# A delta-rule attention and SiLU feed-forward kernel: chunk 0's queries turned two batches ahead of their scores, V loaded one transfer later, joins, narrowing and first MLP pieces in another order

## The chip, the cores and the metric

The kernel runs on one core of one Trainium2 chip. A core has a matrix engine (TensorE, PE in the profile), a vector engine (VectorE, DVE), a scalar engine (ScalarE, ACT), a general engine (GpSimd, POOL) and SyncE (SP), which in this kernel issues nearly all transfers between memory (DRAM) and the core's on-chip memory. TensorE writes into accumulation banks (PSUM); the other engines copy from there. Each engine works through its own instructions in the order in which the program pinned them, and waits where an operand is not ready. The metric is the device time of one execution in microseconds (us); lower is better.

## The reference: what is computed

There are 4 batches of 8 heads, 768 tokens of 48 values each. Per head a state of 48 x 48 values runs over the tokens; keys are scaled to length one.

```python
for t in range(S):
    kt, vt, bt = (k_n[:, :, t], v[:, :, t], beta[:, :, t, None])
    y[:, :, t] = np.einsum('bhd,bhde->bhe', q[:, :, t], state)
    v_old = np.einsum('bhde,bhd->bhe', state, kt)
    state = state + bt[:, :, :, None] * np.einsum('bhd,bhe->bhde', kt, vt - v_old)
...
h = x @ w_in
g = h * (1.0 / (1.0 + np.exp(-h)))
return (g @ w_out).astype(np.float32)
```

`x` is `y` with the heads of a token side by side: 3072 tokens of 384 values. `w_in` is 384 x 2048, `w_out` 2048 x 384. The inputs of the attention are float32; the two weight matrices come in as float64.

## The kernel before: how the work is tiled and ordered

**Chunks.** The 768 tokens are taken in six chunks of 128. Inside a chunk the token-by-token recurrence becomes matrix work: the key products of the chunk form a triangular matrix for each head, which must be inverted; with the inverse, the value corrections, the outputs and the new state are all matmuls. Each chunk has two halves (`hf`) of 64 tokens, and the batches go in two groups (`g`) of two.

**Chunk 0** is prepared by code of its own. Keys are transposed on TensorE (`turn` with j = 0, L490) and their diagonal blocks multiplied (`first_blocks`, L1274). VectorE computes the key lengths (`norm_steps`); `beta_of` (L351) turns beta; `block_steps` (L435) makes the step sizes `pg`. Then `invert_first` solves 16 x 16 blocks by a chain of small VectorE operations and leaves two transposed tables, `low` (L680) and `up` (L684). While VectorE does that, TensorE makes the key scores of the four batches (`first_score`, L1291) and the query scores (`first_queries`, L1293): the latter transposes the queries of a batch (`turn` with j = 1, whose result ScalarE negates into `kq` at L500) and then multiplies keys by queries (`score`, L519), whose result ScalarE copies into `ap` (L534). GpSimd masks those (L1345).

**Which word stands where.** The loop at L1349 advances the inverse by a step and then runs the words of one entry of a list: `s2` is `first_score(2)`, `q0` is `first_queries(0)`, `b` is a filler matmul (`busy`, L338) that waits for the inverse's step at that place. A filler's result is not used. Since every engine has its own order, the place of a word among the inverse's steps, which are VectorE's, does not matter to TensorE; the order of the words does.

**Joins.** `joins(hf, between)` (L1367) puts the small inverses together in ten stages: `corner`, `turned`, `straight`, and the two merges (`merge_half`, L796), each for both groups. After each stage it calls the next entry of `between`: `sizes_0` finishes VectorE's table of key lengths, `sized` scales V of chunk 0 on GpSimd (L447) and begins a weight piece, `filled(n)` does n steps of narrowing, `begin_next` begins the next piece. The first half's joins are followed by `inner` (L830), `first_outputs` (L874), and then the first MLP matmuls (`hidden`, L1031).

**Weights.** Each matrix is taken in eight pieces of 768 KB. A piece is loaded raw (`fetch_w_in`, L285; `fetch_w_out`, L297) and narrowed from float64 to float32 in three steps: two on ScalarE when it is begun (L226, L227), one on VectorE (L231), and one on VectorE with one on GpSimd (L235, L239). `fill(n)` does n such steps in the order of the pieces.

**Transfers.** All loads stand in one line on SP's queue. `linked` makes a load wait until the load before it in line has landed. `load_v(0)` has eight loads of 96 KB (L191).

**The script.** From L1526 on the order of chunk 0's solving, chunk 1's preparation and the MLP is written out as words: `s` a step of solving chunk 0 and then 1, `f` a step of narrowing, `r` one MLP piece (six matmuls of L1031, or their counterpart in the second layer, L1066), `j` a step of the second half's joins, `T` and `q` turns of chunk 1's keys and queries, `p` chunk 1's scores, `g` and `i` chunk 1's inverse (VectorE, L617 and L622), `l` and `m` key lengths, `t` sums of weights, `b` beginning a piece, `W7`, `w2`, `w3` loads of weights, `v` and `k` loads of V and keys. After the script, chunks 1 to 5 are handled by the loop at L1530, which runs two fixed patterns and is left as it is.

Of the kernel before, what the change touches and what calls it, by code (L numbers as in the profile page):

```python
# [19 lines left out]
def kernel(  # L20
# [20 lines left out]
    T = 32  # L41
# [16 lines left out]
    A, CC, M = deque(("a0", "a1", "a2")), deque(("c0", "c1", "c2")), deque(("m0", "m1"))  # L58
# [51 lines left out]
    def together(*parts):  # L110
        for _ in zip_longest(*parts):
            pass
# [12 lines left out]
    def on(e, hf, g):  # L125

        return HALVES[hf ^ e ^ g]
# [7 lines left out]
    def load_pair(to, src, c, bs):  # L135

        for g in range(bs.start // HB, bs.stop // HB):
            us = slice(HB * g, HB * (g + 1))
            for e, hf in ((g, None), (1 - g, 0), (1 - g, 1)):
                rows = slice(0, P) if hf is None else on(e, hf, g)  # L140
                tokens = slice(c * C, (c + 1) * C) if hf is None else slice(c * C + hf * W, c * C + (hf + 1) * W)
                in_line(nc.sync.dma_start(  # L142
                    out=to[rows, us, :, e, 0:D],
                    in_=src[us, e::2, tokens, :].rearrange("b h t d -> t b h d"),
                ))
# [25 lines left out]
    def linked(fetch, *args):  # L171

        pace.append(line[-1])
        fetch(*args)

    def load_k(c, bs=ALL):
        if c < NCH:
            load_pair(kbufs[c % 2], k, c, bs)
# [5 lines left out]
    def load_v(c):  # L184
        if c < NCH:
            vfs[c] = load.tile([P, 2, B, NP, D], FP32, name="vf", bufs=1)
            for hf in range(2):
                for g in range(2):
                    us = slice(HB * g, HB * (g + 1))
                    for e in range(2):  # L190
                        in_line(nc.sync.dma_start(  # L191
                            out=vfs[c][on(e, hf, g), hf, us],
                            in_=v[us, e::2, c * C + hf * W : c * C + (hf + 1) * W, :].rearrange("b h t d -> t b h d"),
                        ))
# [12 lines left out]
    for e in range(2):  # L207
        for g in range(2):
            to, of = slice(HH * e + HH // 2 * g, HH * e + HH // 2 * (g + 1)), slice(HH // 2 * g, HH // 2 * (g + 1))
# [66 lines left out]
    def fetch_w_in(i):  # L276
        if i in (0, 1, 6):
            raw = mlp.tile([P, SIZE], U32, name="raw", tag="gT", bufs=3)[:]
        elif i < 6:
            raw = room(i // 2 - 1, i % 2)  # L280
        else:
            raw = spare
        raw = raw.rearrange("p (a f) -> p a f", a=NKT)
        src = moe_w_in.rearrange("(a p) f -> p a f", p=P)[:, :, i * WF : (i + 1) * WF].bitcast(U32)
        in_line(nc.sync.dma_start(out=raw, in_=src))  # L285
        raws["in", i] = raw.rearrange("p a (f j) -> p a f j", j=2)
# [47 lines left out]
    def busy(n=1, after=None, how=NoSync):  # L334

        for _ in range(n):
            pw = bank(CC, "pw")
            done = pin(nc.tensor.matmul(  # L338
                pw[:, 0:DM], lhsT=ident[:],
                rhs=states[0][:].rearrange("p u a w -> p (u a w)")[:, 0:DM], start=True, stop=True,  # L340
            ))
            if after is not None:
                behind(done, after, how)
                after = None
# [4 lines left out]
    def beta_of(c):  # L349
        pb = bank(A, "pb")  # L350
        pin(nc.tensor.transpose(  # L351
            pb[:, 0:BH], beta_fm[:, c].rearrange("n s t -> n (s t)"), ident[0:BH, 0:BH]
        ))
        pin(nc.scalar.activation(
            out=beta_tok[:, c, :].rearrange("p (n e) -> p e n", e=2),
            in_=pb[:, 0:BH].rearrange("p (e n) -> p e n", e=2), func=ACTF.Copy,
        ))
# [125 lines left out]
    def turn(c, b, j, room, by_vector=False):  # L483

        if j == 0:
            kq_room(c, b)
        src, kq = (kbufs[c % 2], queries[c] if c < 2 else None)[j][:, b], kqs[c, b]
        pt = bank(room, "pt")
        for p in range(NP):
            pin(nc.tensor.transpose(  # L490
                pt[:, p * C : (p + 1) * C], src[:, p].rearrange("p e w -> p (e w)"), ident[:]
            ))
        ptv = pt[:].rearrange("p (a t) -> p a t", a=NP)
        if j == 1:
            if by_vector:
                pin(nc.vector.tensor_scalar(
                    out=kq[:, :, j, :], in0=ptv, scalar1=-1.0, scalar2=None, op0=ALU.mult
                ))
            else:
                pin(nc.scalar.mul(kq[:, :, j, :], ptv, -1.0))  # L500
        elif by_vector:
            pin(nc.vector.tensor_copy(out=kq[:, :, j, :], in_=ptv))
        else:
            pin(nc.scalar.copy(kq[:, :, j, :], ptv))

    def score(c, b, js, rooms, evacuate):

        g, u = b // HB, b % HB
        if (c, g) not in aps:
            aps[c, g] = {}  # L510
        for j in js:
            if j not in aps[c, g]:
                aps[c, g][j] = work.tile([P, HB, H, W], FP32, name=f"ap{j}", tag=f"ap{j}", bufs=2)
        ap, kq, n = aps[c, g], kqs[c, b], len(js)
        pa = [bank(room, f"pa{e}") for e, room in enumerate(rooms)]
        for p in range(NP):
            for e, hf in ((0, 0), (1, 1), (0, 1), (1, 0)):
                rows, half = slice(W * e, W * e + D), slice(W * hf, W * (hf + 1))
                pin(nc.tensor.matmul(  # L519
                    pa[e][half, p * n * W : (p + 1) * n * W], lhsT=kq[rows, p, 0, half],  # L520
                    rhs=kq[rows, p, js[0] : js[-1] + 1, half], start=True, stop=True,
                ))
        for e in range(2):
            of = pa[e][:, 0 : NP * n * W].rearrange("p (a j t) -> p a j t", a=NP, j=n)
            for i, j in enumerate(js):
                evacuate(j, e, ap[j][:, u, e::2, :], of[:, :, i, :])
# [6 lines left out]
    def by_act(to, of):  # L533
        return pin(nc.scalar.copy(to, of))  # L534
# [755 lines left out]

        score(0, b, (0,), (A, CC), evacuate)  # L1291

    def first_queries(b):  # L1293

        def evacuate(j, e, to, of):
            by_act(to, of)

        turn(0, b, 1, M)
        score(0, b, (1,), (A, CC), evacuate)

    busy(3)
    for b in range(B):
        square(0, b)
# [9 lines left out]
    for b in range(B):  # L1313
        add_squares(0, b)
    beta_of(0)
    for t in xis:
        pin(nc.gpsimd.memset(t, 0.0))
    first_sizes = norm_steps(0)
# [4 lines left out]
    pools["m0"] = pools["m1"] = ctx.enter_context(tc.tile_pool(name="hiddens", bufs=1, space=PSUM))  # L1323
    fetch_w_in(0)
    load_k(1)
    load_v(0)
    fetch_w_in(1)
    for c in range(1, NCH):
        beta_of(c)
    for b in range(2):  # L1330
# [3 lines left out]
    linked(load_q, 1)  # L1334
    fetch_w_in(4)
    linked(fetch_w_in, 3)
    linked(fetch_w_in, 5)
    linked(fetch_w_in, 6)
    begin(("in", 0))
    inv = invert_first(step)  # L1340

# [6 lines left out]

    for n in range(1 + Q):  # L1349
        done = next(inv)  # L1350
        for word in ["s2 s3", "", "q0", "", "q1", "", "q2", "", "", "q3", "", "", "b", "", "", "", "", "", ""][n].split():
            at = int(word[1:] or 0)
            if word[0] == "b":
                busy(1, done, Sync)
            elif word[0] == "s":
                first_score(at)
            elif word[0] == "q":
                first_queries(at)
            else:
                turn(1, at, 0, M)  # L1360
    corner, turned, straight = next(inv)
# [5 lines left out]
    def joins(hf, between=()):  # L1367

        for stage in (
            corner(0, hf), corner(1, hf), turned(0, hf), turned(1, hf), straight(0, hf), merge_half(0, hf, False),  # L1370
            straight(1, hf), merge_half(1, hf, False), merge_half(0, hf, True), merge_half(1, hf, True),
        ):
            yield from stage
            for what in between[:1]:
                what()
            between = between[1:]
# [4 lines left out]
    def filled(n):  # L1381
        return lambda: fill(n)
# [5 lines left out]
    def none():  # L1388
        pass

    together(joins(0, [none, sizes_0, sized, none, filled(2), none, filled(1), none, none, begin_next]))

    pieces = chained(hidden(0, 0), hidden(0, 1), project())

# [129 lines left out]
                pieces = chained(feed_forward(1, 0), feed_forward(1, 1))  # L1524

    for text in (  # L1526
        "s f2 s T f T s q b q T j5 j5 j16 f r j5 j8 j4 j16 j5 r q j20 b T f j8 j4 q W7 r j4 f2 j4 b j4 f j4 r j4 f2 j32 r e b j12 j8 f j4 j4 j4 j4 r j4 f j99 l h f2 l s b w2 f r l r l p r s w3 r l p r l2 p f l7 f2 s l b l f p r l5 s f l r l3 p f s2 l2 f l4 p f r2 f p g b p i v l p r f i r i2 r i l r i r b i2 r2 f b r i r3 i r f i b r2 i3 b b i2 r2 f2 i2 f r i r3 i r2 i r2 i r2 f i2 f i f r2 i f b f i4 r i b i r k f r z i r s r2 t r b z s b r f r m r s m r3 t r f2 t m r t f t m s m b r2 b s m3 r m s r m5 b c s m r m2 t s m r m t m2 b m2 r s m2 t m2",
    ):
        script(text)
    for c in range(1, NCH):  # L1530
# [59 lines left out]
```

## Time and profile before

| | |
|---|---|
| time, median of 3 runs | 656.09 us (652.70 to 657.33) |
| the profiled execution | 655.41 us |
| its span (first to last instruction) | 653.5 us |
| mean TensorE clock granted, as a share of full | 0.969 |
| busy: TensorE / VectorE / ScalarE / GpSimd | 631.4 / 391.6 / 216.2 / 95.4 us |
| moved by DMA | 53.68 MB, 82 GB/s on average |

Times in the profile count from the start of the span. A matmul of float32 shows as two records, each with a weight load. A row of the timeline gives start, duration, engine, line, operation, written tile `<-` read tiles, shape and count, and in brackets the idle time of that engine just before it with what ended it; "issue" means that nothing in the profile explains the idle time. In a row that merges several instructions the duration is that of the group. "SPq" is SP's queue: its rows are the issuing of transfers, not their landing. Tile names are those of the program's buffers, which are reused: `w_out<-in_moe_w_in_dram` is a raw piece of `w_in` parked in room that later holds `w_out`.

### The profile page before, as it was taken

How to read it: one execution, taken by the hardware profiler on the slowest of the kernel's cores; microseconds unless marked ns; L12 is line 12 of the kernel's file. 1: busy time of each engine (PE TensorE's matmuls, PEld its weight loads, DVE VectorE, ACT ScalarE, POOL GpSimd, SP SyncE). 2: the span in 40 equal slices, each digit the busy share in tenths (PEclk: the TensorE clock that was granted, in tenths of full speed). 3: DMA queues.
4: the chain of work that ended last, by engine and by line, in shares of the span. 5: the costliest groups of instructions: out<-in, count | busy, mean ns of one | idle time of the engine just before them, and what ended most of it. 6: DMA issues, size and time to landing. Idle time of an engine off the chain costs nothing.

```text
span 653.5 us, 21807 instructions
## 1 busy us (share of the span) xinstructions
PE 631.4 (97%) x9644; PEld 553.4 (85%) x9644; DVE 391.6 (60%) x902; ACT 216.2 (33%) x505; POOL 95.4 (15%) x96
## 2 busy tenths in 40 slices
PE   6879999999999999999999999999999999899997
PEld 4668788766789988989989989989989989789997
DVE  5844988997764986453987453987455964103112
ACT  1545847133342122451122452122451122341111
POOL 5232642146001020010020010020002000000000
PEclk9557999999999999999999999999999999999999
DMA  9763545340278424178424168424163024100101
GB/s 174 167 155 100 175 111 138 73 121 2 52 151 141 66 74 59 37 144 132 73 72 59 47 136 142 61 77 57 35 142 74 17 67 49 40 14 1 25 0 25
DMA packets 141310, 53.68 MB, mean 82 GB/s; under 512 B 112912, under 2 KB 134672, under 8 KB 141216
## 3 DMA queue, kind: packets, MB, share of 16 engines
q1 hardware_dynamic: 140880, 52.14, 39.4%
q8 instruction: 76, 1.25, 0.9%
q10 hardware_dynamic: 336, 0.15, 0.1%
q14 instruction: 18, 0.15, 0.1%
HBM read 39.62 MB, written 10.49 MB: 77 GB/s over the span
## 4 chain that ended last, share of the span: by engine, by line
PE 73%; DVE 9%; DMA 8%; SPq 5%; ACT 2%; issue 1%; POOL 0%; POOLq 0%; DVEq 0%
PE phid L1031 28%; PE px L1138 13%; PE py L1138 9%; PE po L1066 7%; DVE rank L617 4%; DVE x L622 3%; PE pz L830 3%; PE pa L519 3%; SPq L142 2%; DMA w_out<-in_moe_w_in_dram 2%; PE pu L850 2%; PE ph L818 2%; PE pyc L909 2%; DVE sums_of_g L1120 1%; DMA up<-x 1%
## 5 line engine op out<-in xcount | busy, mean ns | idle before, releaser
L1031 PE MATMUL phid<-xT,w_in 128*128 128x256 f32 x1152 | 258.4, 382 | 1.9 <-DMA xT<-part 1.9
L1031 PEld LDWEIGHTS phid<-xT,w_in 128*128 128x128 f32 x1152 | 215.8, 190 | 33.3 <-issue 3.5
L1041 ACT ACTIVATE gT<-phid 128x512 f32<-128x512 f32 x88 | 52.6, 597 | 145.8 <-PE phid L1031 143.6
L617 DVE SCALAR_TENSOR_TENSOR rank<-g,step,x 128x31 f32<-128x31 f32 (+15 forms) x124 | 49.7, 401 | 38.1 <-DMA g<-blocks 34.6
L1120 DVE TENSOR_TENSOR sums_of_g<-gT 128x384 f32<-128x384 f32 (+1 forms) x60 | 30.6, 529 | 58.4 <-ACT gT L1041 47.8
L1138 PE MATMUL py<-w_out,sums_of_g 128*128 128x192 f32 x320 | 56.8, 329 | 0.0
L1138 PE MATMUL px<-sums_of_w,sums_of_g 128*128 128x192 f32 x320 | 56.8, 329 | 0.0
L1138 PEld LDWEIGHTS px<-sums_of_w,sums_of_g 128*128 128x128 f32 x320 | 52.2, 190 | 0.5
L1138 PEld LDWEIGHTS py<-w_out,sums_of_g 128*128 128x128 f32 x320 | 52.2, 190 | 0.4
L622 DVE TENSOR_TENSOR x<-x,rank 128x31 f32<-128x31 f32 (+15 forms) x124 | 42.5, 343 | 4.3
L457 POOL TENSOR_TENSOR vf<-vf,n_slot 128x768 f32<-128x768 f32 x10 | 15.0, 1510 | 174.2 <-DMA vf<-in_v_dram 126.5
L478 DVE STREAM_TRANSPOSE kq<-stage 128x512 f32<-128x512 f32 x28 | 28.4, 1109 | 9.3 <-DMA stage<-in_q_dram 9.3
L534 ACT COPY xT<-pyc 48x128 f32<-48x128 f32 (+2 forms) x126 | 32.7, 260 | 1.6
L1138 PE MATMUL px<-sums_of_w,gT 128*128 128x192 f32 x160 | 28.4, 329 | 0.0
L1138 PE MATMUL py<-w_out,gT 128*128 128x192 f32 x160 | 28.4, 329 | 0.0
L1138 PE MATMUL px<-w_out,gT 128*128 128x192 f32 x160 | 28.0, 327 | 0.0
L830 PEld LDWEIGHTS pz<-vf,xi 64*64 64x64 f32 x768 | 25.0, 142 | 3.2 <-issue 2.9
L540 POOL COPY g<-x 64x256 f32<-64x256 f32 x4 | 5.0, 1242 | 152.6 <-DVE x L625 152.6
L519 PEld LDWEIGHTS pa<-kq 48*64 48x64 f32 x768 | 21.2, 161 | 7.0 <-ACT kq L500 4.4
L519 PE MATMUL pa<-kq 48*64 48x128 f32 (+1 forms) x768 | 24.3, 287 | 2.7 <-ACT kq L500 2.7
L1138 PEld LDWEIGHTS px<-w_out,gT 128*128 128x128 f32 x160 | 26.4, 190 | 0.5
L855 DVE TENSOR_TENSOR state<-state,pu 128x384 f32<-128x384 f32 x22 | 11.2, 551 | 26.0 <-PE pu L850 25.9
(197 smaller groups left out, 859.3 us busy)
## 6 DMA issues: line engine op xcount, KB each, us to landing
vf<-in_v_dram SPq DMA_DIRECT2D x48, 96.0 KB, 3.0
out_dram<-o SPq DMA_DIRECT2D x42, 96.0 KB, 2.2
w_out<-in_moe_w_in_dram SPq DMA_DIRECT2D x4, 768.0 KB, 5.4
sums_of_w<-in_moe_w_out_dram SPq DMA_DIRECT2D x4, 768.0 KB, 5.9
blocks<-ap SPq DMA_DIRECT2D x40, 64.0 KB, 1.9
g<-blocks SPq DMA_DIRECT2D x5, 512.0 KB, 3.5
kb<-in_k_dram SPq DMA_DIRECT2D x12, 192.0 KB, 4.4
kb<-in_k_dram SPq DMA_DIRECT2D x24, 96.0 KB, 4.5
```

The costliest lines, as they stand in the source:

```text
L457: pin(nc.gpsimd.tensor_tensor(out=vf, in0=vf, in1=of, op=ALU.mult))
L478: pin(nc.vector.transpose(out=kqs[c, b][:, :, j, :].rearrange("p a (i m) -> p a m i", i=T), in_=src.rearrange("p a (m d) -> p a m d", d=D) ...
L519: pin(nc.tensor.matmul(pa[e][half, p * n * W : (p + 1) * n * W], lhsT=kq[rows, p, 0, half], rhs=kq[rows, p, js[0] : js[-1] + 1, half], sta ...
L534: return pin(nc.scalar.copy(to, of))
L617: pin(nc.vector.scalar_tensor_tensor(out=tv, in0=g[:, 0:m, m : m + 1].to_broadcast([P, m, n]), scalar=step[:, m : m + 1], in1=x[:, m : m + ...
L622: yield pin(nc.vector.tensor_tensor(out=x[:, 0:m, m:T], in0=x[:, 0:m, m:T], in1=tv, op=ALU.add))
L830: yield pin(nc.tensor.matmul(pz[rows, n * D : (n + 1) * D], lhsT=xis[g][rows, u * H + 2 * p + e, :], rhs=vfs[c][rows, hf, g * HB + u, p, : ...
L1031: pin(nc.tensor.matmul(ph[:, j * GT : (j + 1) * GT], lhsT=w_in[:, a, (2 * f + j) * P : (2 * f + j + 1) * P], rhs=xTs[c, hf][:, a, :], star ...
L1041: pin(nc.scalar.activation(out=hidden_of(c, hf, f), in_=ph[:], func=ACTF.Silu, scale=-0.5 if in_blocks(c) else 0.5))
L1066: pin(nc.tensor.matmul(pos[i][:, 0:DM], lhsT=hidden_of(0, hf, f // 2)[:, at : at + C], rhs=w_outs[f // HFF][:, f % HFF, :], start=(f == 0) ...
L1120: pin(nc.vector.tensor_tensor(out=sums_of_g[:, k, fs], in0=of[0], in1=of[1], op=op))
L1138: pin(nc.tensor.matmul(to, lhsT=at, rhs=quarter(f, *b) if isinstance(b, tuple) else sums_of_w[b][:, f], start=start and f == 0, stop=f == ...
```

## The change

Six edits, all in the order of work; no operation is added or removed.

- `first_queries` is split into two words: `u` turns a batch's queries, `w` scores them. The words now run `s2 u0 u1 w0 s3 u2 w1 u3 w2 w3`.
- The filler that stood after the query scores (word `b`) is gone; one filler is put before the key lengths, behind `beta_of(0)`.
- Piece 1 of `w_in` is loaded ahead of V, where it stood behind V.
- Piece 6 of `w_in` is loaded ahead of piece 5.
- In the first half's joins the calls between the stages move: the lengths and V's scaling one stage later, one narrowing step from behind the second `straight` to behind the first of the last two merges, and the beginning of the next piece from the end to behind the second of the first two merges.
- The script's words stand in another order; it has two more `r` and one `b` less.

```diff
-    def first_queries(b):
-
-        def evacuate(j, e, to, of):
-            by_act(to, of)
-
-        turn(0, b, 1, M)
-        score(0, b, (1,), (A, CC), evacuate)
...
     beta_of(0)
+    busy(1)
...
     fetch_w_in(0)
     load_k(1)
+    fetch_w_in(1)
     load_v(0)
-    fetch_w_in(1)
...
     linked(fetch_w_in, 3)
+    linked(fetch_w_in, 6)
     linked(fetch_w_in, 5)
-    linked(fetch_w_in, 6)
...
-        for word in ["s2 s3", "", "q0", "", "q1", "", "q2", "", "", "q3", "", "", "b", "", "", "", "", "", ""][n].split():
+        for word in ["s2 u0", "u1", "w0", "s3 u2", "w1", "u3", "", "w2 w3", "", "", "", "", "", "", "", "", "", "", "", "", "", "", ""][n].split():
...
-            elif word[0] == "q":
-                first_queries(at)
+            elif word[0] == "u":
+                turn(0, at, 1, M)
+            elif word[0] == "w":
+                score(0, at, (1,), (A, CC), lambda j, e, to, of: by_act(to, of))
...
-    together(joins(0, [none, sizes_0, sized, none, filled(2), none, filled(1), none, none, begin_next]))
+    together(joins(0, [none, none, sizes_0, sized, filled(2), none, none, begin_next, filled(1), none]))
...
-        "s f2 s T f T s q b q T j5 j5 j16 f r j5 j8 j4 j16 j5 r q j20 b T f j8 j4 q W7 r j4 f2 j4 b j4 f j4 r j4 f2 j32 r e b j12 ...
+        "s f2 s T f T s q s q T j5 j16 j8 f j5 f r q T j20 j5 b r j8 j4 j16 j5 j4 q W7 r j4 j4 f2 b r j4 f2 j4 j4 j32 r f e j12 ...
```

More of the change, by code (lines that the diff above doesn't have):

```diff
@@ L1350 @@
         done = next(inv)
-        for word in ["s2 s3", "", "q0", "", "q1", "", "q2", "", "", "q3", "", "", "b", "", "", "", "", "", ""][n].split():
+        for word in ["s2 u0", "u1", "w0", "s3 u2", "w1", "u3", "", "w2 w3", "", "", "", "", "", "", "", "", "", "", "", "", "", ""][n].split():
             at = int(word[1:] or 0)
@@ L1354 @@
                 busy(1, done, Sync)
+            elif word[0] == "n":
+                busy(1)
             elif word[0] == "s":
                 first_score(at)
-            elif word[0] == "q":
-                first_queries(at)
+            elif word[0] == "u":
+                turn(0, at, 1, M)
+            elif word[0] == "w":
+                score(0, at, (1,), (A, CC), lambda j, e, to, of: by_act(to, of))
             else:
@@ L1526 @@
     for text in (
-        "s f2 s T f T s q b q T j5 j5 j16 f r j5 j8 j4 j16 j5 r q j20 b T f j8 j4 q W7 r j4 f2 j4 b j4 f j4 r j4 f2 j32 r e b j12 j8 f j4 j4 j4 j4 r j4 f j99 l h f2 l s b w2 f r l r l p r s w3 r l p r l2 p f l7 f2 s l b l f p r l5 s f l r l3 p f s2 l2 f l4 p f r2 f p g b p i v l p r f i r i2 r i l r i r b i2 r2 f b r i r3 i r f i b r2 i3 b b i2 r2 f2 i2 f r i r3 i r2 i r2 i r2 f i2 f i f r2 i f b f i4 r i b i r k f r z i r s r2 t r b z s b r f r m r s m r3 t r f2 t m r t f t m s m b r2 b s m3 r m s r m5 b c s m r m2 t s m r m t m2 b m2 r s m2 t m2",
+        "s f2 s T f T q s q T j5 j16 j8 f j5 f r q T j20 j5 b r j8 j4 j16 j5 j4 q W7 r j4 j4 f2 b r j4 f2 j4 j4 j32 r f e j12 b j8 j4 j4 f j4 j4 r j4 f j99 l h f2 b l s w2 f r2 l2 p r s w3 r p r l p f l2 f l3 f l3 s l b f l p l2 r l3 s l f l2 r l2 p f s2 l2 f l p l3 f r2 f p v l g p i p r f r i3 l i r2 i r b r f i2 r2 b i r2 i b b i2 r b i r2 i2 f b i4 r3 f r3 f2 r i2 r3 i r f r2 f i2 f i3 b r2 f i f b i r b i2 r i f k r f z i b r2 s r2 t z s b r3 s m2 r4 t f t m f r t m2 s r2 t b s m2 r m2 s r2 m2 b r c m2 s r m2 t m2 s m2 b m f m t m t r m r m4 s",
     ):
```

## The prediction

> **What bounds the kernel now.** I read the page first: its summary, the slices and the shares of the chain of waits.
>
> ```profile
> span 653.5 us, 21807 instructions
> PE 631.4 (97%) x9644; PEld 553.4 (85%) x9644; DVE 391.6 (60%) x902; ACT 216.2 (33%) x505; POOL 95.4 (15%) x96
> ...
> PE   6879999999999999999999999999999999899997
> ...
> PEclk9557999999999999999999999999999999999999
> ...
> PE 73%; DVE 9%; DMA 8%; SPq 5%; ACT 2%; issue 1%; POOL 0%; POOLq 0%; DVEq 0%
> ```
>
> TensorE carries the end. From the fourth slice of 16.3 us on it is at nine tenths or more; what is left lies in the first three slices, where it is not full and its clock is at half. So I asked for the table of stretches there, for three microseconds in which TensorE is never idle, and for two single ones in which the mean clock is neither half nor full.
>
> ```profile
> 10.00:20.00 10.00, 5.22 (x192) 4.48 (x193) 8.66 (x28) 1.88 (x9) 2.83 (x5) 0.76 1.13 196
> 20.00:30.00 10.00, 8.63 (x167) 6.28 (x160) 9.04 (x30) 6.07 (x15) 2.26 (x2) 0.50 0.66 157
> 30.00:40.00 10.00, 8.63 (x236) 6.49 (x237) 3.30 (x7) 3.11 (x8) 5.22 (x5) 0.50 0.85 170
> 40.00:50.00 10.00, 5.59 (x264) 5.14 (x263) 6.01 (x17) 4.92 (x11) 2.23 (x2) 0.50 0.53 159
> 57.00:648.00 591.00, 586.67 (x8504) 517.49 (x8504) 358.00 (x807) 194.41 (x455) 75.33 (x63) 1.00 0.37 74
> ...
> 19.00:22.00 3.00, 3.00 (x66) 2.02 (x62) 2.56 (x11) 1.92 (x6) 0.00 (x0) 0.50 0.82 153
> ...
> 15.00:16.00 1.00, 0.17 (x1) 0.05 (x1) 0.88 (x4) 0.20 (x1) 0.00 (x0) 0.63 1.42 202
> 56.00:57.00 1.00, 1.00 (x8) 0.85 (x8) 0.56 (x2) 0.72 (x2) 0.00 (x0) 0.89 0.57 209
> ```
>
> After each stretch's length stand the busy times of TensorE, its weight loads, VectorE, ScalarE and GpSimd, then clock, DMA share and GB/s. From 57 to 648 us TensorE lacks 4.3 of 591 us. From 10 to 50 us it lacks 11.9 of 40, and runs at half clock: a mean of 0.63 puts the drop at 15.26 us, a mean of 0.89 puts the return at 56.22. Whatever makes the dense part begin earlier therefore moves the end by nearly as much, as long as the other engines keep up. All edits but the last line of the script lie ahead of that part.
>
> **The queries, two batches ahead.** TensorE's rows in order of time (start, duration, operation; in brackets the idle time before it and who ended it):
>
> ```profile
> 22.21 1.99 PE L519 MATMUL pa<-kq 48*64 48x64 f32 x64
> 24.13 1.11 PE L490 MATMUL pt<-ident,z 128*128 128x128 f32 x4
> 25.93 1.13 PE L519 MATMUL pa<-kq 48*64 48x64 f32 x32 [0.69 <-ACT kq L500]
> 26.99 1.11 PE L490 MATMUL pt<-ident,z 128*128 128x128 f32 x4
> ...
> 34.51 1.13 PE L519 MATMUL pa<-kq 48*64 48x64 f32 x32 [0.69 <-ACT kq L500]
> 35.57 1.65 PE L338 MATMUL pw<-state,ident 128*128 128x384 f32 x2
> 37.15 1.05 PE L707 MATMUL pl<-sums_of_w,ap 32*32 32x16 f32 x64
> ...
> 25.28 0.60 ACT L500 ACTIVATE kq<-pt 128x512 f32<-128x512 f32 x1 [0.38 <-PE pt L490]
> ```
>
> Four times TensorE transposes a batch's queries (L490), waits while ScalarE negates them into `kq` (L500), and scores them (L519). One round is 26.99 - 24.13 = 2.86 us, 0.69 of it the wait. Then comes the filler matmul of L338, and at 37.15 the joins begin with L707.
>
> In the new order another batch's score or turn stands between a turn and its own score: about 1 us of TensorE over ScalarE's 0.6. The four waits go: 4 x 0.69 = 2.8 us. The filler goes from here too: 37.15 - 35.57 = 1.6 us. From 22.21 to 37.15 are 14.9 us; 14.9 - 2.8 - 1.6 = 10.5, so the joins would begin at 32.8 instead of 37.15, **4.4 us earlier**. ScalarE has room: in the stretches from 20 to 30 and from 30 to 40 us it is busy 6.1 and 3.1 of 10. The two banks of the turns are enough, since the third turn needs the first one's bank some 3 us after it was written.
>
> What is late next are VectorE's two transposes, which make `low` and `up`:
>
> ```profile
> 28.96 1.05 DVE L680 STREAM_TRANSPOSE sums_of_w<-sums_of_w 128x512 f32<-128x512 f32 x1
> 29.88 1.91 DVE L684 STREAM_TRANSPOSE sums_of_w<-sums_of_w 128x1024 f32<-128x1024 f32 x1
> ```
>
> The corners need `low`, there at 30.0; `turned` needs `up`, at 31.8. Both are ready, so 30.0 is how far this step could go at best: 7.1 us.
>
> **The filler's new place** is behind the transpose of beta, ahead of `pg`:
>
> ```profile
> 14.95 0.21 PE L351 MATMUL pb<-ident,beta_fm 32*128 32x32 f32 x1
> 17.23 0.61 PE L435 MATMUL pg<-pick,spread 128*128 128x32 f32 x2 [2.07 <-DVE spread L413]
> ```
>
> TensorE idles 2.07 us there for `spread`. A filler of 1.65 from 15.16 ends at 16.8, before 17.23: nothing, with 0.4 us to spare. Without that cover it would push `pg`, the step sizes and the whole inverse by at most 1.65; but `up` has a us to spare, so the joins would hardly see it. It starts only 0.1 us before the clock drops, too late to hold it.
>
> **Joins and narrowing.** The joins' rows, with the instruction fetches of that stretch:
>
> ```profile
> 42.50 0.73 PE L723 MATMUL pl<-sums_of_w 32*32 32x32 f32 x19 [2.12 <-issue]
> ...
> 46.23 0.91 PE L736 MATMUL pl<-sums_of_w 32*32 32x32 f32 x52 [1.27 <-issue]
> ...
> 49.68 1.33 PE L796 MATMUL px<-xi,xe_y 32*32 32x32 f32 x32 [1.02 <-DVE xe_y L537]
> 50.94 3.54 PE L830 MATMUL pz<-vf,xi 64*64 64x48 f32 x62
> ...
> q8 instruction: 3, 0.05, 2.1%
> ...
> 48.20 0.96 DVE L235 SCALAR_TENSOR_TENSOR w_in<-raw,w_in 128x768 uint32<-128x768 uint32 x1
> 51.32 0.89 ACT L226 ACTIVATE w_in<-w_out 128x768 f32<-128x768 f32 x1
> 52.11 0.97 ACT L227 ACTIVATE w_out<-w_out,plus 128x768 int32<-128x768 uint32 x1
> ```
>
> The joins last from 37.15 to 50.94, 13.8 us. Two waits in them, 2.12 and 1.27, have no releaser; I read them as instruction supply, because three blocks of 16 KB (0.05 MB) are fetched between 36 and 48 us and 52 of these matmuls take only 0.91 us. The Trainium skill, "Runtime: NRT & Kernel Launch", section "Instruction fetch mechanics", says that an engine's instructions come in 16 KiB blocks of 256 and that crossing a boundary is mostly hidden. The block size agrees with the row; that it is hidden does not, if these waits are fetches. By the page nothing of the stage would hang on them and the two waits would go with some other cause, for a sum 3.4 us lower.
>
> The change leaves the number of TensorE instructions as it is, so the boundaries stay at the same matmuls. Their price is bounded by none (3.4 us won) and by one more wait of 2.1 lost; I take no change, as the same DMA queue is loaded in both places.
>
> The third wait, 1.02, is VectorE's: the narrowing step L235 (0.96) stands before the copy that TensorE needs. It moves behind the second merge, so 1.0 goes. Against it, ScalarE's narrowing of the third piece (0.89 + 0.97 = 1.86) moves ahead of its last two copies into `xi`, on which `inner` (L830) waits. Those copies would end some 4.5 us after the matmul that begins at 46.23 here, and `inner` begins 4.7 after it: **0.2 us** won, between 1.0 won and 0.9 lost. Behind `inner` ScalarE is then free for its first copy, 0.3 won. The sizes and V's multiply move one stage back, into the wait that the fetch makes: nothing; without that cover 1.5 on GpSimd, still ahead of `inner` by several us.
>
> **Transfers.** SP issues them in order:
>
> ```profile
> 18.13 6.18 SPq L191 DMA_DIRECT2D vf<-in_v_dram  x8
> 24.35 0.62 SPq L285 DMA_DIRECT2D raw<-in_moe_w_in_dram  x1
> 29.23 0.37 SPq L285 DMA_DIRECT2D w_out<-in_moe_w_in_dram  x1
> 41.16 1.48 POOL L447 TENSOR_TENSOR vf<-vf,n_slot 128x768 f32<-128x768 f32 x1 [2.13 <-DVE xe_y L537]
> ```
>
> Piece 1 takes 29.23 - 24.35 = 4.9 us to land. Issued ahead of V it delays V's issue by 0.6 us and shares the engines with it, so V lands by 29 to 32, against a first use at 41.2, in the new order about 38. Cover gone only if V came 6 us late. The chain behind (pieces 2, 4, 3) starts from V's landing in place of piece 1's: between 1 us earlier and 2 later; pieces 5 and 6 change places, 4 us later for 5, which is used last of the two. I take nothing.
>
> **The script.** The number of fills, joins and solving steps stays, two more MLP steps stand before the end of the piece list, and TensorE changes between MLP matmuls and others as often as before (22 runs of MLP work in both). I take 0, between 1 won and 2.7 lost (the limit of the second rival).
>
> Sum: 4.4 + 0.2 + 0.3 = **4.9 us**. The profiled execution took 655.41 us, 1.9 more than its span; that makes 650.5. The median of the three runs, 656.09, is 0.7 higher. I say 650.8.
>
> **Rivals.**
> *Earlier clock* (0.22). Between 50.94 and 56.22 the dense work runs at half clock, 5.3 us for 2.6 us of work. If the denser queries or the earlier `inner` bring the full clock back by the time `inner` begins, 2.6 us more go: about 648. For it: without the four waits TensorE would have no gap of its own from 22 to 35 us. Against it: from 19 to 22 us it is busy 3.00 of 3 now and the clock stays at 0.50. The Trainium skill, "TensorE: Matmul & The Clock Gate", Part 1, says the clock returns after about 3.4 us of sustained work and falls after an idle window of 3.413 us; the distance from drop to return, 40.96 us, is twelve such windows, so the trace agrees on the window, not on the short way back. By the page alone the return would come near 26 us and this rival would be the forecast.
>
> *Swallowed at the first merges* (0.18). VectorE's inverse of chunk 1 must be done before TensorE's merges:
>
> ```profile
> 100.00:140.00 40.00, 39.91 (x234) 30.19 (x225) 36.78 (x78) 14.91 (x22) 7.71 (x6) 1.00 0.43 105
> 138.90 1.99 DVE L595 STREAM_TRANSPOSE xe_y<-sums_of_w 128x1024 f32<-128x1024 f32 x1
> 143.62 1.22 PE py L772 x82
> ```
>
> `xe_y` is there at 140.9 and used at 143.6: 2.7 us to spare, and VectorE is busy 36.8 of 40. If VectorE doesn't come earlier at all, the gain ends at 2.7: 652.7 to 653. Against it: the chain starts from TensorE's work, so it moves with it.
>
> *Slower: the clock returns late* (0.12). Half clock goes on until TensorE has had enough unbroken work. If the joins and `inner` now have a gap in each such stretch, the dense part begins at half clock. With `inner` at 46.4, the work done at time T is (T - 46.4)/2; before it was 2.64 + T - 56.22. They are equal at T = 60.8: from there each us costs half a us. A return at 65 makes it 2 us slower, 658; one later than 74 makes it 1% slower.
>
> *No effect on the joins* (in the range of the forecast): if instruction supply alone paced the joins, `inner` would move by what the fetches move, 2 to 4 us.
>
> **Numbers.** Forecast 0.48 (649 to 653), earlier clock 0.22 (646 to 649), swallowed 0.18 (652 to 655), late clock 0.12 (655.5 up). The range 646 to 656.5 leaves out some 0.15. One per cent, 6.6 us, is about what a measurement here can tell from no change: faster takes the earlier clock and a little of the forecast, 0.27; slower the far end of the late clock and what I don't see, 0.08; the rest 0.65.
>
> **What would show it.** The query scores without a wait on ScalarE's `kq`; L707 at 32 to 33; the two waits without releaser at the same matmuls, near 38 and 42; L830 near 46; the clock's return not later than 56; from 57 on the same rows 5 us earlier. Wrong would be: waits on `pt`'s banks, L707 still near 37, a return of the clock after 61, or a wait at the merges of chunk 1.

## The result, and the profile after

Over 20 runs each the changed kernel takes 653.19 us at the median (649.22 to 655.84), the kernel before 657.38 (652.70 to 659.85): a ratio of 0.9931, 95% interval 0.9911 to 0.9950, or some 4.5 us faster. Both kernels spread by 6 to 7 us from one execution to the next. The two profiled executions differ by less, 651.4 against 653.5 us of span, since the one of before took 655.41 us, less than its kernel's median; so the traces are compared stage by stage, and the times by the medians.

The page of the changed kernel and its table of stretches:

```profile
span 651.4 us, 21809 instructions
...
PE   6859999999999999999999999999999999899997
...
PEclk9758999999999999999999999999999999999999
...
20.00:30.00 10.00, 9.68 (x250) 7.38 (x242) 8.97 (x31) 8.52 (x21) 1.94 (x2) 0.74 0.73 163
30.00:40.00 10.00, 5.29 (x294) 4.88 (x295) 7.01 (x17) 2.95 (x7) 6.90 (x6) 0.60 0.67 151
40.00:50.00 10.00, 6.16 (x200) 5.82 (x201) 3.91 (x8) 4.96 (x11) 1.82 (x1) 0.50 0.60 170
...
52.00:53.00 1.00, 1.00 (x23) 0.88 (x18) 0.50 (x1) 0.86 (x2) 0.00 (x0) 0.72 1.03 403
57.00:648.00 591.00, 585.06 (x8386) 516.43 (x8384) 358.26 (x805) 191.82 (x449) 73.96 (x62) 1.00 0.38 75
```

The dense part is as dense as before, 585 of 591 us. The change is ahead of it. From 20 to 30 us TensorE is busy 9.7 of 10 where it had 8.6, and its mean clock is 0.74 where it had 0.50. At half clock up to the return and full clock after it, that puts the return at 25.2 us, and by the next row (0.60) the clock stays full until 32.1. From 30 to 40 us it is emptier than before, 5.3 against 8.6. The clock comes back for good at 52.6 (mean 0.72 in that microsecond) in place of 56.2.

TensorE's rows in order of time, for the queries and the joins:

```profile
23.60 1.88 PE L490 MATMUL pt<-ident,z 128*128 128x128 f32 x8
25.40 1.16 PE L519 MATMUL pa<-kq 48*64 48x64 f32 x64
28.29 1.45 PE L519 MATMUL pa<-kq 48*64 48x64 f32 x64
30.47 1.30 PE L707 MATMUL pl<-sums_of_w,ap 32*32 32x16 f32 x128 [0.72 <-DVE sums_of_w L680]
...
36.89 0.74 PE L723 MATMUL pl<-sums_of_w 32*32 32x32 f32 x21 [2.84 <-issue]
...
41.44 0.92 PE L736 MATMUL pl<-sums_of_w 32*32 32x32 f32 x53 [2.08 <-issue]
...
46.69 0.95 PE L796 MATMUL px<-xi,xe_y 32*32 32x32 f32 x26 [2.38 <-issue]
47.57 3.54 PE L830 MATMUL pz<-vf,xi 64*64 64x48 f32 x62
...
56.55 1.56 PE L1031 MATMUL phid<-xT,w_in 128*128 128x256 f32 x6
```

The scores no longer wait for ScalarE. The joins begin at 30.47, 6.7 us earlier than the 37.15 of before, and they begin with a wait on VectorE's `low` (L680). But they last 17.1 us where they took 13.8: the waits without releaser are three, 7.3 us together, where they were two and 3.4. So `inner` (L830) begins 3.4 us earlier, at 47.57, and the first MLP matmul 3.6 earlier, at 56.55 against 60.12 in this row of before:

```profile
60.12 1.56 PE L1031 MATMUL phid<-xT,w_in 128*128 128x256 f32 x6
```

In this pair of executions half of what the queries won was lost in the joins. The experiments ask which edit wins the rest, and what the waits without releaser are.

### The profile page after: what moved, and what is told of

It reads as the page before. It is cut to its first block, busy times and chain, and to the rows that moved or that the text cites. A ratio compares the mean times of both kernels' runs of the same rounds, so it can differ in the third digit from the quotient of the medians.

```text
span 651.4 us, 21809 instructions
## 1 busy us (share of the span) xinstructions
PE 627.3 (96%) x9644; PEld 550.7 (85%) x9644; DVE 394.3 (61%) x902; ACT 216.3 (33%) x505; POOL 95.7 (15%) x96
## 4 chain that ended last, share of the span: by engine, by line
PE 85%; DVE 8%; DMA 2%; issue 2%; ACT 1%; SPq 1%; POOL 0%; DVEq 0%; POOLq 0%
PE phid L1031 35%; PE px L1138 15%; PE py L1138 11%; PE po L1066 7%; PE pa L519 3%; PE pz L830 3%; DVE rank L617 2%; PE pu L850 2%; PE ph L818 2%; DVE x L622 2%; PE pyc L909 2%; PE pt L490 1%; PE pyc L896 1%; PE px L772 1%; PE py L772 1%
## 5 line engine op out<-in xcount | busy, mean ns | idle before, releaser
L1041 ACT ACTIVATE gT<-phid 128x512 f32<-128x512 f32 x88 | 52.6, 598 | 143.6 <-PE phid L1031 140.8
L478 DVE STREAM_TRANSPOSE kq<-stage 128x512 f32<-128x512 f32 x28 | 28.6, 1114 | 8.1 <-DMA stage<-in_q_dram 7.6
L830 PEld LDWEIGHTS pz<-vf,xi 64*64 64x64 f32 x768 | 25.2, 142 | 3.2 <-issue 2.9
L830 PE MATMUL pz<-vf,xi 64*64 64x48 f32 x768 | 26.9, 226 | 0.0
L1138 PEld LDWEIGHTS py<-w_out,gT 128*128 128x128 f32 x160 | 26.1, 190 | 0.3
L1138 PEld LDWEIGHTS px<-sums_of_w,gT 128*128 128x128 f32 x160 | 26.1, 190 | 0.2
```

Of the source, the lines that this page charges most:

```text
L478: pin(nc.vector.transpose(out=kqs[c, b][:, :, j, :].rearrange("p a (i m) -> p a m i", i=T), in_=src.rearrange("p a (m d) -> p a m d", d=D) ...
L830: yield pin(nc.tensor.matmul(pz[rows, n * D : (n + 1) * D], lhsT=xis[g][rows, u * H + 2 * p + e, :], rhs=vfs[c][rows, hf, g * HB + u, p, : ...
L1041: pin(nc.scalar.activation(out=hidden_of(c, hf, f), in_=ph[:], func=ACTF.Silu, scale=-0.5 if in_blocks(c) else 0.5))
L1138: pin(nc.tensor.matmul(to, lhsT=at, rhs=quarter(f, *b) if isinstance(b, tuple) else sums_of_w[b][:, f], start=start and f == 0, stop=f == ...
```

## The experiments

Ratios are to the kernel before, run on the same chip in the same series, with 95% intervals. The changed kernel's own ratio, 0.9931, comes from the series of the result, and each kernel has one profiled execution.

**1. The query order alone.** The kernel before with the new words and the filler's new place:

```diff
     beta_of(0)
+    busy(1)
...
-        for word in ["s2 s3", "", "q0", "", "q1", "", "q2", "", "", "q3", "", "", "b", "", "", "", "", "", ""][n].split():
+        for word in ["s2 u0", "u1", "w0", "s3 u2", "w1", "u3", "", "w2 w3", "", "", "", "", "", "", "", "", "", "", "", "", "", ""][n].split():
```

> The kernel before with the new order of the query words and the filler in its new place; transfers, joins and script as before. My theory (the query order carries the gain): the joins' first matmul (L707) near 30.5 us as in the changed kernel, waits without releaser in the joins longer than the 3.4 us of before, the inner matmuls (L830) 3 to 4 us earlier than 50.94, the time 3 to 4.5 us below before, ratio about 0.994. Rival (the gain needs the new joins and script as well): L707 early too, but ratio within 0.998 to 1.002.

Measured: 0.9924 (0.9898 to 0.9950), median 651.27 us. Its joins, which begin at 30.07 with a wait of 0.84 us on `low`, in order of time from the next wait on:

```profile
31.46 1.37 PE L707 MATMUL pl<-sums_of_w,ap 32*32 32x16 f32 x88 [0.87 <-issue]
35.84 0.75 PE L723 MATMUL pl<-sums_of_w 32*32 32x32 f32 x21 [1.67 <-issue]
39.84 0.92 PE L736 MATMUL pl<-sums_of_w 32*32 32x32 f32 x53 [1.53 <-issue]
43.30 0.42 PE L796 MATMUL px<-xi,xe_y 32*32 32x32 f32 x6 [1.02 <-DVE xe_y L537]
45.64 0.95 PE L796 MATMUL px<-xi,xe_y 32*32 32x32 f32 x26 [1.93 <-issue]
46.52 3.54 PE L830 MATMUL pz<-vf,xi 64*64 64x48 f32 x62
```

The whole gain is there without any other edit. The four waits without releaser sum to 6.0 us, and the three of the changed kernel's places among them to 5.1, so they don't come from the new joins or transfers either. The wait of 1.02 on VectorE, which the new joins remove, is still there, and the wait of 1.93 that follows it six records later is the likely reason why its removal wins nothing.

**2. Everything but the queries.** The changed kernel with the old words and the filler in its old place.

```diff
     beta_of(0)
-    busy(1)
...
-        for word in ["s2 u0", "u1", "w0", "s3 u2", "w1", "u3", "", "w2 w3", "", "", "", "", "", "", "", "", "", "", "", "", "", ""][n].split():
+        for word in ["s2 s3", "", "q0", "", "q1", "", "q2", "", "", "q3", "", "", "b", "", "", "", "", "", ""][n].split():
```

> The changed kernel with the query words and the filler back in their old order and place. My theory: L707 near 37 us, L830 within 1 us of 50.9, ratio 0.998 to 1.003. Rival (joins and script carry the gain): ratio 0.994 to 0.996.

Measured: 1.0015 (0.9989 to 1.0042); L707 at 35.95, L830 at 50.67 against 50.94. Joins, transfers and script together are worth nothing that can be measured. The wait of 1.02 on VectorE is gone here, and a third wait without releaser stands in its place, though TensorE comes only 1.2 us earlier than before:

```profile
49.84 0.90 PE L796 MATMUL px<-xi,xe_y 32*32 32x32 f32 x26 [2.37 <-issue]
```

In this execution the clock was full from 25.1 to 28.5 us, with the old order of the queries.

**3 and 4. One edit back at a time.** The changed kernel with the script of before, and the changed kernel with the transfers of before:

```diff
-    fetch_w_in(1)
     load_v(0)
+    fetch_w_in(1)
...
-    linked(fetch_w_in, 6)
     linked(fetch_w_in, 5)
+    linked(fetch_w_in, 6)
```

> The changed kernel with the script of before. My theory (script worth nothing): the same time as the changed kernel within 1.5 us, ratio about 0.993, first MLP matmul near 56.5 us. Rival (the script wins up to 1 us or loses some of the gain): the end of the span against the first MLP matmul differs by more than 1 us from the changed kernel's 594.8.

> The changed kernel with V ahead of piece 1 and piece 5 ahead of piece 6 again. My theory (the transfers' order is worth nothing): ratio about 0.993; L830 within 1 us of 47.6. Rival (the new order of transfers made the waits without releaser longer, 7.3 in place of 3.4 us, because the fetches of instructions meet other transfers): these waits sum to under 5 us here and the time is 2 us lower, ratio 0.990.

Measured: 0.9918 (0.9890 to 0.9947) with the old script, first MLP matmul at 56.12, and 594.9 us from there to the end of the span against 594.8; 0.9934 (0.9911 to 0.9957) with the old transfers, L830 at 46.44, four waits without releaser of 6.9 us together. Both rivals fall.

**5. Are the waits the supply of instructions?** Sixteen tiny matmuls are put behind the early filler, their results unused:

```diff
     beta_of(0)
     busy(1)
+    pt0 = bank(CC, "pw")
+    for n in range(16):
+        pin(nc.tensor.matmul(
+            pt0[0:T, T * n : T * (n + 1)], lhsT=ident[0:T, 0:T], rhs=ident[0:T, 0:T], start=True, stop=True,
+        ))
+    pt0 = bank(CC, "pw")
+    pt0 = bank(CC, "pw")
```

> The changed kernel with 16 tiny matmuls (32x32, results unused) behind the early filler: 64 more instructions of TensorE, weight loads among them, ahead of the joins. My theory (the waits without releaser in the joins are the supply of instructions, in blocks of 256): each comes 32 matmul records earlier in the program: the first before about the sixth of the L723 matmuls of turned in place of the 38th, the second within the first 25 or so of straight in place of its middle, the third 32 records ahead of where it was in the merges. Rival (they are waits on data or on a bank that the profile doesn't name): they stay before the same matmuls.

It has one run, of 653.9 us, and is read for its waits alone:

```profile
35.32 1.57 PE L723 MATMUL pl<-sums_of_w 32*32 32x32 f32 x52 [1.32 <-issue]
39.99 0.74 PE L796 MATMUL py<-xe_y,ap 32*32 32x32 f32 x21 [2.07 <-issue]
44.92 1.80 PE L796 MATMUL px<-xi,xe_y 32*32 32x32 f32 x58 [2.52 <-issue]
```

Counted in matmul records from the first L707 on, the three waits of the changed kernel stand behind records 166, 294 and 422; in experiment 1 and in the runs with one edit back they stand at the same three. They are 128 records apart, 256 instructions with the weight loads. Experiments 1 and 4 have one more, behind record 40. With 32 records more ahead, they stand behind 135, 262 and 390: 31 or 32 earlier, each. They follow the count of instructions and not the data. (My guess of where the second would fall, in `straight`, was a miscount: it is in the merge, L796.) The waits are shown to be the boundaries of instruction blocks. The transfers in the traces agree: the instruction queue (q8) brings 76 packets of 16 KB, room for 19456 instructions, where TensorE has 19288, and in all 14 profiled executions each of these waits ends 1.1 to 1.7 us after one of these packets has landed. For the changed kernel they land at 35.36, 40.23 and 45.31 us, and the waits end at 36.89, 41.44 and 46.69.

**6 and 7. What sets their length?** The loads from piece 2 on (experiment 6), or those behind piece 2 (experiment 7), wait for the last matmul of the joins. So nothing else is loaded during the joins in experiment 6, and next to nothing from 36 us on in experiment 7, where piece 2 is still landing until then.

```diff
-    linked(fetch_w_in, 2)
-    linked(load_q, 1)
-    fetch_w_in(4)
-    linked(fetch_w_in, 3)
-    linked(fetch_w_in, 6)
-    linked(fetch_w_in, 5)
...
     together(joins(0, [none, none, sizes_0, sized, filled(2), none, none, begin_next, filled(1), none]))
+    pace.append(pins[mybir.EngineType.PE])
+    load_q(1)
+    linked(fetch_w_in, 2)
+    linked(fetch_w_in, 4)
+    linked(fetch_w_in, 3)
+    linked(fetch_w_in, 6)
+    linked(fetch_w_in, 5)
```

In experiment 7 `linked(fetch_w_in, 2)` stays in its place, and `fetch_w_in(4)` follows `load_q(1)` as in the changed kernel.

> The changed kernel in which chunk 1's queries and pieces 2 to 6 of w_in wait for the last matmul of the joins, so that no data is being loaded in most of the joins (piece 2 is then begun later, in the script). Theory (fetches of instructions queue behind other transfers): the three waits without releaser, 7.3 us in the changed kernel, fall to 4 or less and L830 comes 3 us earlier, near 44. Rival (a fetch takes this long whatever else moves): the waits stay at 6.5 to 7.5 and L830 near 47. The total time says little here, since the pieces come some 12 us later; 0 to 8 us slower than the changed kernel.

> The changed kernel in which piece 2 is loaded as before, but chunk 1's queries and the pieces 4, 3, 6 and 5 wait for the last matmul of the joins. Theory (fetches queue behind other transfers): the second and third wait without releaser, 2.1 and 2.4, fall below 1.5 each, L830 near 45, the time 0 to 2 us below the changed kernel if the later pieces are not missed. Rival (a fetch takes as long anyway): L830 near 47 and the time up to 2 us above.

Experiment 6, then experiment 7:

```profile
37.70 0.92 PE L736 MATMUL pl<-sums_of_w 32*32 32x32 f32 x53 [1.29 <-issue]
41.58 0.95 PE L796 MATMUL px<-xi,xe_y 32*32 32x32 f32 x26 [1.00 <-issue]
42.45 3.54 PE L830 MATMUL pz<-vf,xi 64*64 64x48 f32 x62
66.75 0.43 PE L736 MATMUL pl<-sums_of_w 32*32 32x32 f32 x12 [6.42 <-ACT xe_y L534]
```

```profile
33.88 0.74 PE L723 MATMUL pl<-sums_of_w 32*32 32x32 f32 x21 [0.58 <-issue]
37.61 0.92 PE L736 MATMUL pl<-sums_of_w 32*32 32x32 f32 x53 [1.26 <-issue]
41.22 0.95 PE L796 MATMUL px<-xi,xe_y 32*32 32x32 f32 x26 [0.73 <-issue]
```

The waits fall to 2.3 and 2.6 us, and `inner` begins at 42.45 and 42.18, 5 us earlier than in the changed kernel. That fits a fetch which is slower while other transfers run, but it is not shown: experiment 11 below has 1.7 us of waits with transfers running. The packets themselves take 0.9 to 1.7 us in every execution. What differs is when the next one starts: 1.1 and 1.3 us after the end of a wait in experiment 6, where nothing else moves, and 1.0 to 3.4 us in the others. The pause does not pay: the pieces come late (6.42 us of waiting at 66.75 in experiment 6, for a copy that stands behind ScalarE's narrowing of a piece), and the ratios are 1.0085 (1.0060 to 1.0110) and 0.9984 (0.9953 to 1.0016); for experiment 7 that misses the expected 0 to 2 us below the changed kernel.

**8. Small packets.** Chunk 1's queries move behind piece 4:

```diff
     linked(fetch_w_in, 2)
+    linked(fetch_w_in, 4)
     linked(load_q, 1)
-    fetch_w_in(4)
-    linked(fetch_w_in, 3)
+    fetch_w_in(3)
```

> The changed kernel with chunk 1's queries (small packets) loaded behind piece 4 in place of ahead of it. Theory (it is the many small packets that delay the fetches): the first two waits without releaser together below 3.5 us in place of 4.9, L830 1.5 us earlier, ratio to before 0.990 to 0.992. Rival (any transfer delays them alike): waits as in the changed kernel within 0.7 us, ratio 0.992 to 0.994.

Measured: waits of 0.92, 1.26 and 1.00 us, L830 at 43.21, first MLP matmul at 52.97, 3.6 us ahead of the changed kernel, and yet 0.9924 (0.9897 to 0.9952). By 99 us the lead is gone: the long run of MLP matmuls begins at 98.78 where the changed kernel has 98.82. The table of stretches shows a part of where:

```profile
70.00:75.00 5.00, 3.83 (x101) 3.25 (x102) 4.58 (x8) 4.11 (x6) 4.73 (x6) 0.84 0.69 205
75.00:80.00 5.00, 5.00 (x60) 3.75 (x61) 3.79 (x4) 1.23 (x3) 4.20 (x4) 0.82 0.29 116
```

The clock is at half for 3.4 us there, from 73.4 to 76.8, right after a wait without releaser of 1.2 us; such waits sum to 2.7 us between 53 and 99, in place of 0.9. Whether it was the small packets is not settled: the waits in the joins differ between kernels with the same transfers (see experiments 10 and 12).

**9. The filler alone.** The kernel before with the filler in its new place and nothing else:

```diff
     beta_of(0)
+    busy(1)
...
-        for word in ["s2 s3", "", "q0", "", "q1", "", "q2", "", "", "q3", "", "", "b", "", "", "", "", "", ""][n].split():
+        for word in ["s2 s3", "", "q0", "", "q1", "", "q2", "", "", "q3", "", "", "", "", "", "", "", "", ""][n].split():
```

> The kernel before with nothing changed but the filler, which moves from behind the query scores to behind the transpose of beta. My theory (1.6 us of the joins' earlier start is the filler's, 2.8 the four waits'): L707 1.6 us earlier, at 35.5 to 36; but the instruction blocks pace the joins, so L830 within 1.5 us of before and ratio 0.997 to 1.001. Rival (the filler's place is the gain): ratio 0.994 or less.

Measured: 0.9957 (0.9942 to 0.9973): between what the theory and the rival expected, and more than half of the change's gain. L707 comes at 35.55, 1.6 us earlier as expected, but the profiled execution shows L830 at 50.49 only, with waits of 1.30 and 3.18 us, and it was among the slowest of its nine (656.29 us; the median is 654.71). So the gain is shown by the times, and what became of it in a typical execution isn't seen in this one. No run has the new order of the queries with the filler in its old place. What the order alone is worth is therefore only the difference between this run and experiment 1, 0.9957 against 0.9924, and their intervals overlap (from 0.9942 to 0.9950).

**10. No filler.** The changed kernel without the early filler:

```diff
     beta_of(0)
-    busy(1)
```

> The changed kernel without the early filler, 4 instructions of TensorE less ahead of the joins. My theory (it only fills an idle stretch): L707 near 30.3 as in the changed kernel, the waits without releaser two matmul records later in the joins, ratio 0.992 to 0.995. Rival (the filler keeps the clock up or brings it back early): the clock doesn't return near 25 us, L707 at 32 or later.

```profile
30.21 1.30 PE L707 MATMUL pl<-sums_of_w,ap 32*32 32x16 f32 x128 [0.74 <-DVE sums_of_w L680]
...
35.26 0.69 PE L723 MATMUL pl<-sums_of_w 32*32 32x32 f32 x19 [1.46 <-issue]
38.99 0.91 PE L736 MATMUL pl<-sums_of_w 32*32 32x32 f32 x52 [1.31 <-issue]
42.87 0.85 PE L796 MATMUL px<-xi,xe_y 32*32 32x32 f32 x24 [1.01 <-issue]
...
20.00:30.00 10.00, 9.35 (x241) 7.05 (x234) 9.01 (x31) 8.76 (x22) 2.20 (x2) 0.77 0.80 171
```

0.9913 (0.9887 to 0.9939). The waits stand two records later, as they should, and the clock comes back as in the changed kernel (mean 0.77 from 20 to 30 us). The filler in its new place does nothing that can be measured; what counts is that it is gone from the old one. Note that the three waits sum to 3.8 us here, with the changed kernel's transfers, where its own profiled execution had 7.3: their length differs by 3.5 us between two executions that differ in the early filler alone. The shorter joins are not kept here either: the first MLP matmul comes at 53.16, 3.4 us ahead of the changed kernel, but the clock is at half again from 72.5 to 79.3 us, and the span of 652.6 us is longer than the changed kernel's 651.4.

**11 and 12. Can both kernels be beaten?** Chunk 1's queries behind piece 4 as in experiment 8, once in the kernel of experiment 1, once in that of experiment 3.

> The query order alone (kernel before with the new words and the filler's new place) and chunk 1's queries loaded behind piece 4: an attempt at a better version. Theory (waits without releaser in the joins are worth their time): L830 near 43, first MLP matmul near 52.5, and 2 us below the query order alone: ratio 0.989 to 0.991. Rival (as in the run with chunk 1's queries late, the gain is given back before 99 us to waits without releaser and a stretch of half clock): ratio 0.992 to 0.994.

> The changed kernel with the script of before and chunk 1's queries loaded behind piece 4. Theory (the script of the change is what gives the earlier start back): ratio 0.988 to 0.991. Rival (it is given back whatever the script): 0.992 to 0.994, with waits without releaser between 53 and 99 us of 2 us or more in place of 0.9.

Measured: 0.9892 (0.9866 to 0.9918; median 649.25 us) and 0.9930 (0.9908 to 0.9953). The first is the lowest of all, and in its execution the lead stays: first MLP matmul at 52.87 against 55.50 in experiment 1, which has the same script, and the long run of MLP matmuls at 94.64 against 97.02. Its waits without releaser in the joins sum to 1.7 us. Its interval just overlaps that of the changed kernel, so that it beats it is likely and not shown. The second, with 5.4 us of waits in the joins in spite of the late queries, gains nothing on experiment 3. Its ratio lies in the rival's range, but not for the rival's reason: between 53 and 99 us its waits without releaser are 0.6 us.

## Why the prediction was right, point by point

The forecast was 650.8 us within 646 to 656.5, a gain of 4.9 us by its sum (650.8 lies between the 650.5 of the profiled execution and the 651.2 that its own step to the median would give); measured were 653.19 and a gain of 4.2 between the medians, 4.5 by the ratio. That the sum came so near is partly luck: two of its terms were off in opposite directions.

- **What bounds the kernel: right in the main.** From the dense part on, the start decides most. From the first MLP matmul to the end of the span are 594.8 us; before, 653.48 - 60.12 = 593.4. Of the 3.6 us at that matmul 2.1 are left at the end in this pair. The rest went in small waits that differ from execution to execution: 0.9 us in place of 0.3 without a releaser before 99 us, 0.8 in place of 0.4 at later merges. With the old script the stretch is 594.9 us, so the script isn't the cause; with the query order alone it is 593.9. A still earlier start was not kept: of the 3.6 and 3.4 us that the first MLP matmul is ahead of the changed kernel in experiments 8 and 10, 1.6 and nothing are left at the end of the span, with the clock at half for 3.4 and 6.8 us behind 72 us. In experiment 11, where the clock stays full, 2.1 of 2.6 us are left against experiment 1.
- **The queries' waits: right, the size too small.** Gone are the four waits of 0.69 and the filler, and L707 comes 6.7 us earlier where the term said 4.4. The sum was worked out at half clock throughout; the clock was full from 25.2 us on, which was the mechanism of the first rival. Experiment 9 shows the filler's 1.6 us in the trace, as priced (L707 at 35.55); the other 5.1 us of the step are the order's and the clock's together. In the times the filler's move alone is worth more than half of the gain. What the step named as next late, `low`, is what the joins now wait for (0.72 <-DVE L680).
- **The filler's new place at nothing: right.** `pg` still waits 0.87 us for `spread`:

```profile
17.56 0.60 PE L435 MATMUL pg<-pick,spread 128*128 128x32 f32 x2 [0.87 <-DVE spread L413]
```

- **Joins: the reading of the waits was right, their price was not.** They are instruction blocks (experiment 5). The term "I take no change" measured 3.9 us more in this pair, beyond the 2.1 that it allowed for loss; in experiment 10, with the same joins and transfers, it is 0.4. The step looked at the two boundaries that were exposed in before, and not at a third one six records behind VectorE's wait. It comes out when that wait is taken away, as in experiment 2 (2.37), and also when TensorE merely arrives sooner, as in experiment 1 (1.93). What makes the waits longer in one execution than in another stays open.
- **The 0.2 of the narrowing's order: swallowed** by that third boundary, within the same merge. That ScalarE's narrowing ahead of the copies cost nothing has probably the same reason. The 0.3 behind `inner` isn't seen by itself: from there to the first MLP matmul are 8.98 us in place of 9.18.
- **Transfers and script at nothing: right** (experiments 2, 3 and 4).
- **Earlier clock: half of it.** The clock came back at 25.2 us, early as this rival has it, but its condition asked for full clock when `inner` begins (47.57), and the clock had fallen again at 32.1, early in the joins. What it won, it won in the queries. The order of the queries is not its only cause, since in experiment 2 the old order had full clock from 25.1 to 28.5 too. Experiments 6 and 7 end the joins 5 us sooner still, and the clock is at half there too.
- **Swallowed at the first merges: no.** VectorE moved along, 138.90 to 135.76, and TensorE did not wait ahead of these merges:

```profile
135.76 1.99 DVE L595 STREAM_TRANSPOSE xe_y<-sums_of_w 128x1024 f32<-128x1024 f32 x1
...
141.98 1.22 PE py L772 x82
```

- **No effect on the joins (instruction supply alone): not far off.** `inner` moved by 3.4 us, within the 2 to 4 of this rival, and the three long waits of the joins are the supply of instructions.
- **Late clock: no.** It came back at 52.6, and 60.8 was the point from which it would have decided.

The chance of one per cent or more, 0.27, stood against a gain of 0.7%.

On the rule that crossing an instruction boundary is mostly hidden (the Trainium skill, "Runtime: NRT & Kernel Launch", "Instruction fetch mechanics"): the block of 256 instructions agrees with the 128 records between two waits; "mostly hidden" does not hold in these joins, where the waits at the boundaries are 0.5 to 3.2 us each. On the clock (the Trainium skill, "TensorE: Matmul & The Clock Gate", Part 1): the early return that it would give did come with the denser queries, between 22.3 and 28.6 us in every profiled execution with the new order. In the changed kernel it came behind 3.41 us (21.84 to 25.25) in which TensorE was busy throughout; but the 3.41 us before them were as full, and the clock stayed at half. The fall within the joins does not agree: the 3.41 us ahead of it (28.67 to 32.08) hold 2.31 us of work and are no idle window.

## What to carry to other kernels

Where an engine turns an operand and then waits for another engine to hand it back, put another unit of the same work between the two, and look for filler work that stands in front of real work. Before a gain is claimed for the stage behind, count that stage's instructions: a stage of very short matmuls can be paced by the supply of its instructions, and then part of an earlier start may be paid back as longer waits. Such waits have no releaser in the profile and stand at a fixed count of instructions; adding a few dull instructions ahead of them shows what they are.

## What the runs showed of the hardware

- TensorE's waits without releaser in the joins stood 128 matmul records (256 instructions) apart, give or take two, in every run, and moved by 31 or 32 records when 32 were put ahead of them. Each cost 0.5 to 3.2 us and ended 1.1 to 1.7 us after a 16 KB packet of the instruction queue had landed.
- Their sum over the stage was 2.3 us with no other transfer running, 2.6 with next to none from 36 us on, 3.8 to 7.3 in the changed kernel's order of transfers, and 1.7 to 5.4 with chunk 1's queries loaded late. That other transfers lengthen them is likely and not shown.
- In all profiled executions with the new query order the clock was full for a while within the queries and at half again within the joins; it came back only behind them, between 46.8 and 52.6 us.
